# The last two blocks' down projection by two levels of seven products

## The chip, the cores and the metric

The kernel runs on one core of one Trainium2 chip. The metric is the device time of one execution in microseconds (us). TensorE (PE; PEld is its weight load), VectorE (DVE), ScalarE (ACT), GpSimd (POOL) and the queue engine SyncE (SP) each work through their own list of instructions and wait for each other by semaphores.

## The reference

The kernel computes a linear attention followed by a gated feed-forward block, all in float32:

```
kv  = einsum('bhsd,bhse->bhde', k, v)            # 8 batches, 8 heads, 576 rows, 64 wide
o   = einsum('bhsd,bhde->bhse', q, kv)
o   = o / sqrt(mean(o*o, -1) + 1e-6) * g_norm
x   = o as (4608 tokens, 512)
g   = x @ w_gate                                 # 512 x 1536
out = (g * sigmoid(g) * (x @ w_val)) @ w_out     # 1536 x 512
```

The product with `w_gate` and `w_val` is called *up* here, the one with `w_out` *down*; `h` is what lies between them.

## The kernel before, in words

The 4608 tokens are cut into nine blocks of 512. Blocks 0, 1 and 2 go alone; blocks 3 to 8 go in three pairs (`Pair`), of which 7 and 8 are the last. The attention of later blocks is worked in between, so that in the last pair nothing but up and down is left.

**Products by seven.** A 2 x 2 split of both factors needs seven products of half the size in place of eight, at the price of sums of the parts (the form of Winograd, whose parts are named S1, S3 and so on in the code). The seven are numbered 1, 5, 6, 2, 7, 4, 3. `CHAIN` says into which bank of PSUM each one accumulates: 1, 6, 7 and 4 run on one after the other in a bank of pool b, 2 has one in a, 5 and 3 share one in c. After every product the state of its bank is copied or added into SBUF, and the next product of the chain may only then overwrite it. Pool b has three banks, c two, a one, m two.

**Up of a pair** uses two levels, 49 products per column j of `h` (six columns, `NP`), for both blocks at once. The outer seven are taken in four groups (`Inner.GROUPS`: (1,5), (6,2), (7), (4,3)), and each group runs the inner seven in the order of `Inner.sequence`, with two products of the group before among its own. An inner product of a group of two is two matmuls of 128 x 128 weights against 256 columns (128 tokens of each block). VectorE adds it into SBUF, or ScalarE copies it (`Inner.multiply`, matmul at L816, copies at L830). `made1` to `made3` make the outer sums on POOL, the Silu on ScalarE (L845, L862), and `h` by two multiplications on POOL (L132 through `mul`), for the last column on VectorE. `Ffn.h_sums` then makes the sums of `h` that down needs, on POOL, for the first block of the pair. The names `add`, `sub` and `mul` stand in L130, L131 and L132, so all sums of the kernel have one of these lines.

**Weights of up** are made ready during blocks 1 and 2, written to DRAM as `w`, and read back by `Stream` (L906, SP queue) into `t` tiles, nine of 256 KB, each about as long ahead as tiles come free.

**Down** uses one level, block after block (`Down`, matmul at L661, the last product's at L1032 through `third`). Here `h` is held as weights and `w_out` (`wo`) is moved: a product is 12 matmuls of 128 x 128 against 256 columns, and the result has tokens in its rows, as `out` wants it. Three of the seven need differences of parts of `wo`, which POOL makes into `t` tiles (`turn_t`). For the last pair (`down.lone`) the order is 1, 5, 6, 2, 7, 3, 4, and for the very last block (`final`) results are added and stored in halves, so that the last piece is small. Stores are issued on SP (L1122).

**What sets the order.** The code is traced once, and a scheduler orders each engine's instructions, as a rule in the order of the code, but with those moved ahead that are ready before others. `tc.issue_after` and `in_order(engines)` tie it down; down of a pair stands in `in_order(nc.tensor.engine)`, so only TensorE's order is fixed there.

Of the kernel before, what the change touches and what calls it, by code (L numbers as in the profile page):

```python
# [18 lines left out]
def kernel(  # L19
# [620 lines left out]
    class Quad:  # L640


        def __init__(self, steps):
            self.steps = steps
            self.ps, self.room = {}, None

            self.apart = {}

# [3 lines left out]
        def multiply(self, p):  # L652
            name, first = CHAIN[p]
            if first:
                tiles = [PSUMS[name].tile([P, 2, HB], F32, name=name) for _ in range(1 + (name in self.apart))]
                self.ps[name], self.apart[name] = tiles[0], tiles[-1]
            banks = self.ps[name], self.apart[name]
            for e, i in self.order(p):
                lhsT, rhs = self.operands(p, e, i)

                self.ffn.multiplied = nc.tensor.matmul(  # L661
                    banks[e][:, e], lhsT=lhsT, rhs=rhs, start=first and i == 0 and (e == 0 or banks[0] is not banks[1]),
                    stop=i == self.steps - 1, skip_group_check=True,
                )
            getattr(self, f"after{p}", lambda: None)()
# [91 lines left out]
    class Inner:  # L757
# [94 lines left out]
        def made3(self, p, e, q):  # L852
# [7 lines left out]
            mul(engine, h[:, :, :, 0:HB], halves(c11), halves(c12))  # L860
            with tc.issue_after(self.ffn.fifth.ins):
                nc.scalar.activation(out=c21, in_=c21, func=ACT.Silu)  # L862
            mul(engine, h[:, :, :, HB:BLK], halves(c21), halves(c22))
            self.ffn.ended = self.ffn.a.h_sums(self.j, 1, engine)

# [13 lines left out]
    class Stream:  # L879
# [15 lines left out]
        def pump(self):  # L895

            while self.next and not self.held[-9]:
                n, j, c = key = self.next.pop(0)
                tile_ = t_tile(key)
                os, ps = JOINT[c]  # L900
# [6 lines left out]

        def use(self, n, j, o, p):
            c, i = self.joint[o, p]
            key = n, j, c  # L910
# [74 lines left out]
    class Down(Quad):  # L985
        def __init__(self, ffn):
# [3 lines left out]
            self.final = ffn.n == NB - 1  # L990
            self.lone = False
            self.opens = None
            self.keeps = False
            if self.final:
                self.apart["c"] = None
# [16 lines left out]
        def multiply(self, p, es=(0, 1)):  # L1012
            if p == 3 and self.lone:
                self.third(es)
                return
# [7 lines left out]
        def third(self, es):  # L1023


            if es[0] == 0:
                tiles = [m_psum.tile([P, 2, HB], F32, name="m") for _ in range(1 + self.final)]
                self.thirds = tiles[0], tiles[-1]
            for e in es:
                for i in range(self.steps):  # L1030
                    lhsT, rhs = self.operands(3, e, i)
                    self.ffn.multiplied = nc.tensor.matmul(  # L1032
                        self.thirds[e][:, e], lhsT=lhsT, rhs=rhs, start=i == 0 and (e == 0 or self.final),
                        stop=i == self.steps - 1, skip_group_check=True,
                    )
            if not self.final:
                add(nc.vector, self.o1[:, :, HD:DM], self.thirds[0], self.u2)
                self.ffn.store(self.o1, 0)
                return
            for e in es:  # L1040
                add(nc.vector, self.o1[:, e, HD:DM], self.thirds[e][:, e], self.u2[:, e])
                self.ffn.store(self.o1[:, e : e + 1, HD:DM], e, slice(HD, DM))

        def after6(self):
            super().after6()
            if self.lone:
                self.add_c(self.u2, self.u2)

        def order(self, p):
            order = [(e, i) for e in range(2) for i in range(self.steps)]  # L1050
            return order if p == 3 and self.final else sorted(order, key=lambda ei: ei[1])
# [17 lines left out]
        def rows(self):  # L1069
            o = ring()  # L1070
            self.o1, self.o2 = o[:, 0:2], o[:, 2:4]

        def after2(self):
            if self.lone:
                self.rows()
            add(nc.vector, self.o1[:, :, 0:HD], self.ps["a"], self.s)
            if self.final:
                self.ffn.store(self.o1[:, :, 0:HD], 0, slice(0, HD))
# [4 lines left out]
        def after7(self):  # L1083
            if not self.lone:
                self.rows()
            u3 = self.piece(2)
            nc.scalar.copy(out=u3, in_=self.ps["b"])
            self.add_c(self.o2[:, :, HD:DM], u3)
# [5 lines left out]
        def after3(self):  # L1094
            self.add_c(self.o1[:, :, HD:DM], self.u2)
            if not self.final:
                self.ffn.store(self.o1, 0)
                return
            for e in range(2):
                self.ffn.store(self.o1[:, e : e + 1, HD:DM], e, slice(HD, DM))  # L1100

        def add_c(self, o, u):

            if not self.final:
                add(nc.vector, o, self.ps["c"], u)
                return
            for e, c in enumerate((self.ps["c"], self.apart["c"])):
                add(nc.vector, o[:, e], c[:, e], u[:, e])

    class Ffn:  # L1110
# [9 lines left out]
        def store(self, o, t, columns=slice(None)):  # L1120
            rows = out[BLK * self.n : BLK * (self.n + 1), columns].rearrange("(t p) d -> p t d", t=T)
# [40 lines left out]
        def down(self, nxt, then={}):  # L1162
# [3 lines left out]
            down.lone = nxt is None  # L1166
            order = (1, 6, 5, 7, 2, 4, 3) if 5 in fill else (1, 5, 6, 7, 2, 4, 3)
            if down.lone:
                order = (1, 5, 6, 2, 7, 3, 4)
            for p in order:  # L1170
# [305 lines left out]
```

## Time and profile before

| | us |
|---|---|
| median of 3 runs | 1013.13 |
| lowest, highest | 1012.27, 1013.3 |
| the profiled execution, its own time | 1012.7 |
| span of its instructions | 1010.9 |
| last pair, up | 808 to 934.6 |
| last pair, down | 934.6 to 1007.6 |
| PE busy in the span | 993.7 |
| DVE, ACT, POOL busy in the span | 673.7, 232.2, 369.6 |

The span runs from the first to the last instruction; the execution's own time is 1.8 us longer. The granted clock of TensorE is 1.0 throughout. One float32 matmul leaves two records, so counts of matmul records are twice the number of matmuls in the code. A line of a group gives the line in the code, the engine, the operation, what is written and read, the shape and the count, then busy time and mean duration in ns, then the idle time just before and what ended it. A row of busy time by stretches gives the stretch, its length, and the busy time of PE, PEld, DVE, ACT and POOL, with the number of instructions in brackets, then granted clock, share of the DMA engines and GB/s.

### The profile page before, as it was taken

To read this page: it belongs to the slowest core of one execution; us is meant where nothing else is said; L and a number is where in the kernel's file an instruction comes from. 1 tells how busy PE (TensorE), PEld (TensorE's weight loads), DVE (VectorE), ACT (ScalarE), POOL (GpSimd) and SP (SyncE) were. 2 spreads that over 40 slices of the span, in tenths; PEclk is the share of its full clock that TensorE was granted. 3 is DMA by queue.
4 is the path that set the end of the run, shared out by engine and by line. 5 is a ranking of instruction groups with operands and counts; after the bars stand their busy time and mean duration, and the time that the engine had idled before them with its cause. 6 is when DMAs were issued, how large, how long until landed. Compare 5 with 4: busy or idle time off the path is not lost.

```text
span 1010.9 us, 17078 instructions
## 1 busy us (share of the span) xinstructions
PE 993.7 (98%) x6506; PEld 831.6 (82%) x6506; DVE 673.7 (67%) x1121; ACT 232.2 (23%) x367; POOL 369.6 (37%) x290
## 2 busy tenths in 40 slices
PE   5999999999999999999999999999999999999998
PEld 4544688888888888888888888888888888888887
DVE  2999797589868477656676746666668566666311
ACT  2665111221122311212211121121112121121000
POOL 0000263255544240445456004455660026546600
PEclk9999999999999999999999999999999999999999
DMA  8688653483866855767742464667221654553011
GB/s 220 198 266 260 120 93 136 97 288 97 210 136 122 214 114 158 189 179 182 170 130 42 111 164 135 182 164 191 77 42 43 146 164 144 150 145 101 1 42 42
DMA packets 254290, 143.23 MB, mean 142 GB/s; under 512 B 149504, under 2 KB 236544, under 8 KB 254208
## 3 DMA queue, kind: packets, MB, share of 16 engines
q1 hardware_dynamic: 223488, 138.20, 50.8%
q10 hardware_dynamic: 30656, 3.94, 2.5%
q8 instruction: 52, 0.85, 0.4%
q14 instruction: 30, 0.25, 0.1%
q0 software_dynamic: 64, 0.00, 0.0%
HBM read 104.99 MB, written 28.70 MB: 132 GB/s over the span
## 4 chain that ended last, share of the span: by engine, by line
PE 75%; DMA 1%; POOL 0%; SPq 0%; issue 0%; DVE 0%; POOLq 0%
PE b L816 22%; PE b L661 20%; PE c L816 11%; PE c L661 9%; PE a L816 5%; PE a L661 5%; PE m L431 1%; PE m L1032 1%; PE m L370 1%; DMA ld<-in_v_dram 1%; POOL t L131 0%; SPq L312 0%; PE b L370 0%; PE b L431 0%; PE a L431 0%
## 5 line engine op out<-in xcount | busy, mean ns | idle before, releaser
L816 PE MATMUL b<-arena,t 128*128 128x256 f32 x1008 | 244.5, 381 | 0.0
L816 PEld LDWEIGHTS b<-arena,t 128*128 128x128 f32 x1008 | 190.1, 190 | 29.6 <-DVE r L130 2.4
L130 POOL TENSOR_TENSOR r<-r 128x256 f32<-128x256 f32 (+1 forms) x90 | 94.7, 1054 | 246.1 <-DVE r L130 154.9
L130 DVE TENSOR_TENSOR r<-b,r 128x512 f32<-128x512 f32 (+1 forms) x234 | 138.9, 606 | 60.1 <-PE b L816 54.8
L130 DVE TENSOR_TENSOR r<-c,r 128x512 f32<-128x512 f32 (+1 forms) x170 | 104.5, 623 | 81.9 <-PE c L816 40.1
L132 POOL TENSOR_TENSOR arena<-r 128x1024 f32<-128x1024 f32 (+1 forms) x54 | 102.1, 1904 | 112.3 <-DVE r L130 67.9
L131 POOL TENSOR_TENSOR t<-wo 128x512 f32<-128x512 f32 x54 | 76.9, 1445 | 167.8 <-DVE wo L130 105.9
L130 DVE TENSOR_TENSOR r<-a,r 128x512 f32<-128x512 f32 x93 | 59.2, 636 | 108.3 <-PE a L661 70.7
L816 PE MATMUL c<-arena,t 128*128 128x256 f32 x504 | 122.5, 379 | 0.0
L131 DVE TENSOR_TENSOR arena<-arena 128x512 f32<-128x512 f32 (+3 forms) x96 | 104.3, 1101 | 20.0 <-PE b L661 17.7
L816 PEld LDWEIGHTS c<-arena,t 128*128 128x128 f32 x504 | 95.6, 190 | 13.5 <-issue 0.3
L661 PE MATMUL b<-wo,arena 128*128 128x256 f32 x432 | 98.1, 382 | 0.2
L661 PE MATMUL b<-t,arena 128*128 128x256 f32 x432 | 96.2, 379 | 0.0
L661 PEld LDWEIGHTS b<-wo,arena 128*128 128x128 f32 x432 | 81.2, 190 | 12.5 <-DVE arena L132 0.9
L661 PEld LDWEIGHTS b<-t,arena 128*128 128x128 f32 x432 | 82.1, 190 | 11.2
L830 ACT COPY r<-b 128x512 f32<-128x512 f32 x54 | 31.7, 586 | 189.9 <-PE b L816 189.9
L131 POOL TENSOR_TENSOR t<-arena 128x512 f32<-128x512 f32 x36 | 51.1, 1432 | 56.2 <-PE c L661 21.9
L816 PE MATMUL a<-arena,t 128*128 128x256 f32 x252 | 66.1, 379 | 0.0
L816 PEld LDWEIGHTS a<-arena,t 128*128 128x128 f32 x252 | 47.9, 190 | 6.5
L661 PE MATMUL c<-t,s 128*128 128x256 f32 x216 | 48.1, 379 | 0.0
L661 PE MATMUL a<-wo,arena 128*128 128x256 f32 x216 | 48.1, 379 | 0.0
L661 PEld LDWEIGHTS a<-wo,arena 128*128 128x128 f32 x216 | 41.0, 190 | 5.6
(115 smaller groups left out, 1242.9 us busy)
## 6 DMA issues: line engine op xcount, KB each, us to landing
t<-w SPq DMA_DIRECT2D x180, 256.0 KB, 3.1
out_dram<-r SPq DMA_DIRECT2D x17, 512.0 KB, 2.9
ld<-in_k_dram SPq DMA_DIRECT2D x26, 288.0 KB, 4.6
ld<-in_v_dram SPq DMA_DIRECT2D x26, 288.0 KB, 6.1
t<-w SPq DMA_DIRECT2D x54, 128.0 KB, 2.3
ld<-in_moe_w_gate_dram SPq DMA_DIRECT2D x12, 512.0 KB, 4.6
ld<-in_moe_w_val_dram SPq DMA_DIRECT2D x12, 512.0 KB, 4.7
ld<-in_moe_w_out_dram SPq DMA_DIRECT2D x12, 512.0 KB, 4.8
```

Of the source, the lines that this page charges most:

```text
L130: add = lambda e, o, a, b: e.tensor_tensor(out=o, in0=a, in1=b, op=OP.add)
L131: sub = lambda e, o, a, b: e.tensor_tensor(out=o, in0=a, in1=b, op=OP.subtract)
L132: mul = lambda e, o, a, b: e.tensor_tensor(out=o, in0=a, in1=b, op=OP.mult)
L370: self.positions = nc.tensor.matmul(self.kv_ps[r][u * D : (u + 1) * D, g, :], lhsT=k[:, u, c, :], rhs=v[:, u, c, :], start=(c == 0), stop= ...
L431: self.multiplied = nc.tensor.matmul(self.ps[i][u][p : p + D, t, j, :], lhsT=self.qt[rows, tile_t, head, p : p + D], rhs=kvs[b % 3][rows, ...
L661: self.ffn.multiplied = nc.tensor.matmul(banks[e][:, e], lhsT=lhsT, rhs=rhs, start=first and i == 0 and (e == 0 or banks[0] is not banks[1 ...
L816: self.ffn.multiplied = nc.tensor.matmul(ps[:, i], lhsT=stream.use(self.ffn.n, self.j, o, p), rhs=self.operand(o, p), start=first and i == ...
L830: copied = nc.scalar.copy(out=dst, in_=ps)
L1032: self.ffn.multiplied = nc.tensor.matmul(self.thirds[e][:, e], lhsT=lhsT, rhs=rhs, start=i == 0 and (e == 0 or self.final), stop=i == self ...
```

## The change

Down of the last pair is done by two levels for both blocks at once, in the manner of up: 49 products of three matmuls, with a 128 x 128 part of `wo` (or a difference of such parts) as the weights and 128 tokens of each block, 256 columns, moved. The result has the columns of `out` in its rows and tokens along them, and must be turned back.

- *During up of the last pair* VectorE makes the parts of `wo`, by `Deep.tick`, one step after every second product: 6 sums inside `wo` (512 elements in each of 128 partitions), 12 differences for the outer products 1, 2, 6, 3 into `ld` tiles (384 elements), and for the outer products 5, 7, 4 three sets each, of three differences (512, 128 and 256 elements) in one buffer, written to DRAM as `leaf` on SP (448 KB a set).
- *The sums of `h`* are made for both blocks on POOL as columns come out (`Deep.made`), and the inner ones of two columns at a time on VectorE (`turn`). The second half of the last column is put off into down (`second`).
- *Down* (`Deep.down`) writes out by hand the order of products `m(group, inner)`, of the sums for the inner level (`sum_x`, 768 elements each) and the outer level (`outer`, 768 each), and of the results. The groups are (1,2), (6,5), (7), (4,3). It stands in `in_order` for TensorE and VectorE both.
- *Leaf weights* are read back through `Stream`, 192 KB a product, after the pair's own.
- *Turning back.* Two of the four quarters of the result are turned by VectorE in blocks of 32 x 32 and placed by 16 DMAs each of 128 B pieces (`send`), one quarter on ACT's queue and one on SP's. The other two are turned by 16 TensorE transposes in four steps (`turn_back`), copied by ScalarE (the last one by both) and stored.
- *Gone:* `apart`, `final`, `lone`, `third` and `add_c`, which served the old last pair alone.

The diff, cut to its core:

```diff
+            if self.ffn.deep:
+                self.ffn.deep.made(self.j, engine, c21, halves(c21), halves(c22), h)
+                return
...
+    class Last(Inner):
+        GROUPS = ((1, 2), (6, 5), (7,), (4, 3))
...
+            for c in cs:
+                for i, o in enumerate(self.outers):
+                    self.ffn.multiplied = nc.tensor.matmul(
+                        ps[:, i], lhsT=self.deep.weight(o, p, c), rhs=self.deep.operand(o, p, c),
+                        start=first and c == 0 and i == 0, stop=c == 2, skip_group_check=True,
+                    )
...
+            if p in self.ADDED:
+                add(nc.vector, dst, ps, dst)
+            elif self.g == 3:
+                add(nc.vector, dst, ps, self.shared[2][:, :, :, e, q])
+            elif self.g == 0:
+                nc.scalar.copy(out=dst, in_=ps)
+            else:
+                add(nc.vector, dst[:, 0], ps[:, 0], self.onto[:, :, e, q])
+                if n > 1:
+                    nc.scalar.copy(out=dst[:, 1], in_=ps[:, 1])
...
+            for i, o in enumerate(self.LEAVES):
...
+                        lambda b=b, rows=rows, raw=raw: sub(nc.vector, raw, b[:, rows], self.quadrant(6)[:, rows]),
+                        lambda: sub(nc.vector, temp[:, 4], temp[:, 0], temp[:, 1]),
+                        lambda: sub(
+                            nc.vector, temp[:, 5:7], temp[:, 2:4], temp[:, 1:2].to_broadcast([P, 2, P])
+                        ),
+                        lambda i=i, c=c: nc.sync.dma_start(out=self.dram[:, i, c], in_=temp[:, 0:7]),
...
+        def tick(self):
+            self.count += 1
+            if self.later and self.count % 2 == 0:
+                self.later.pop(0)()
+
+        def made(self, j, engine, c21, g, v, h):
+            def second():
+                mul(engine, h[:, :, :, HB:BLK], g, v)
+                a11, a21, a22 = h[:, :, 0, 0:HB], h[:, :, 0, HB:BLK], h[:, :, 1, HB:BLK]
+                add(engine, a21, a21, a22)
+                sub(engine, a21, a21, a11)
...
+            if j == NP - 1:
+                self.second = second
+                return
+            second()
+            if j % 2:
+                self.later[0:0] = self.turn(j // 2, (0, 1))
...
+        def down(self):
...
+            run(self.turn(2, (0,)))
+            m(0, 1, (0, 1))
+            m(0, 2, (0, 1))
+            m(0, 1, (2,))
+            self.sum_x(0, 1, 2)
+            m(0, 2, (2,))
+            m(0, 6)
+            self.sum_x(1, 1, 2)
+            m(0, 5)
+            self.sum_x(2, 1, 2)
+            m(0, 7)
+            self.second()
+            run(self.turn(2, (1,)))
+            self.outer(5, ((0, 0),))
+            m(0, 3)
+            self.outer(5, ((0, 1),))
+            m(1, 1)
...
+            m(2, 5)
+            add(nc.vector, c11, p1, c11)
+            nc.vector.transpose(out=room[:, 0], in_=c11)
+            self.send(room[:, 0], 0, 0, nc.scalar)
+            self.outer(3)
+            m(2, 2)
+            m(2, 7)
...
+            add(nc.vector, v, u2, c22)
+            self.sum_x(0, 4, 3)
+            m(2, 3)
+            m(3, 1)
+            self.sum_x(1, 4, 3)
+            m(2, 4)
+            m(3, 6)
+            self.sum_x(2, 4, 3)
+            m(3, 5)
+            add(nc.vector, c22, u3, c22)
+            nc.vector.transpose(out=room[:, 1], in_=c22)
+            self.send(room[:, 1], 1, 1, nc.sync)
+            m(3, 2)
+            m(3, 7)
...
+            self.turn_back(0, 0)
+            m(3, 3)
+            self.turn_back(1, 1)
+            m(3, 4)
+            self.turn_back(1, 0)
+            self.turn_back(0, 1, True)
...
+        if pair.deep:
+            stream.leaves(pair.deep)
+            pair.up(fill)
+            with in_order(nc.tensor.engine, nc.vector.engine):
+                pair.deep.down()
+            continue
```

## The prediction

> **What bounds the kernel now.** I read the page first, then busy time by stretches for the two stages that the change rewrites, then the chain of waits, then the groups and the timeline for the prices.
>
> ```profile
> PE 993.7 (98%) x6506; PEld 831.6 (82%) x6506; DVE 673.7 (67%) x1121; ACT 232.2 (23%) x367; POOL 369.6 (37%) x290
> ```
>
> TensorE is busy for all but 17 us of the span. The busy time by stretches puts the last pair's up stage in the first row and its down stage in the second:
>
> ```profile
> 808.00:934.60 126.60, 126.60 (x586) 110.91 (x586) 84.66 (x144) 25.71 (x35) 65.54 (x53) 1.00 0.47 141
> 934.60:1007.60 73.00, 72.94 (x338) 63.86 (x337) 16.46 (x21) 5.75 (x9) 16.54 (x13) 1.00 0.07 26
> ```
>
> The columns after the length are PE, PEld, DVE, ACT, POOL. PE never idles in either. In up, VectorE already works 84.7 of 126.6 us and POOL 65.5; in down both have nearly nothing to do. The chain of waits ends so:
>
> ```profile
> 999.77 5.18 PE b L661 x24
> 1004.95 2.60 PE m L1032 x12
> 1007.55 0.02 issue
> 1007.58 0.42 DVE r L130
> ```
>
> One down product is 12 matmuls (24 records) in 5.18 us, **0.432 us per matmul** of 256 columns. Fourteen products are 168 matmuls, 72.6 us of the 72.9 us between 934.64 and 1007.55. Every matmul taken out is therefore worth 0.432 us, provided that VectorE, which gets the new sums, keeps up.
>
> **The prices of VectorE and POOL.** Groups of the up stage, shapes apart:
>
> ```profile
> L130 DVE TENSOR_TENSOR r<-b,r 128x512 f32<-128x512 f32 x53 | 36.6, 691 | 15.2 <-PE b L816 13.9 <-PE a L816 0.5
> L130 DVE TENSOR_TENSOR r<-b,r 128x256 f32<-128x256 f32 x24 | 10.0, 416 | 0.6
> L132 POOL TENSOR_TENSOR arena<-r 128x1024 f32<-128x1024 f32 x10 | 23.4, 2363 | 19.0 <-DVE r L130 19.0
> ```
>
> [...] One behind the other, starts in this trace lie closer: 0.33 us for 256 elements, 0.60 for 512, 1.14 for 1024; so 0.87 for 768[...].
>
> [...] in the up stage of block 1:
>
> ```profile
> 221.88 0.29 DVE L130 TENSOR_TENSOR t<-t 128x128 f32<-128x128 f32 x1
> 222.21 1.70 DVE L131 TENSOR_TENSOR r<-t 128x256 f32<-128x256 f32 x2
> 222.21 1.54 POOL L132 TENSOR_TENSOR arena<-r 128x512 f32<-128x512 f32 x1 [2.18 <-DVE t L130]
> 223.72 1.31 POOL L131 TENSOR_TENSOR t<-wo 128x512 f32<-128x512 f32 x1
> 223.83 1.35 DVE L131 TENSOR_TENSOR t<-t 128x128 f32<-128x128 f32 x1
> ```
>
> The same 128-element subtract takes 0.29 us free and 1.35 us behind POOL's 1.31. Adds that read PSUM and one SBUF tile stay at 0.69 whatever POOL does. [...]
>
> **Down, part by part.** *Removed:* 168 matmuls. *Added:* 49 products of 3 matmuls, 147 x 0.432 = 63.5 us, and 16 TensorE transposes; those of block 0 (L494) start every 0.11 us, so 1.7 us. Bare sum 65.2, **7.7 us less** than 72.9. Against it stand VectorE's own sums. They are 33 of 768 elements (21 in sum_x, 12 in outer: 28.7 us), evacuations of about 12 us, two transposes (L386's 1024-element one: 1.23), seven sums or products of 1024 elements or pairs of 512: some 54 us, against 16.5 before. Both engines' order is fixed here, so a late sum stops TensorE. Walking the written order with these prices, three places don't fit:
> - After product (0,7) VectorE does its evacuation, the postponed second half of h (1024, 512, 512), two turns of 512 and the first outer sum: 0.2+0.6+1.2+4x0.69+0.96 = 5.7 us. TensorE has only product (0,3), 2.6 us, before (1,1) needs that sum: **3.1 us** idle.
> - From product (2,5) to the evacuation of (3,1) VectorE has 0.33+1.14+1.23+4x0.87+2x0.33+1.14+2x0.87+0.33+0.69 = 10.7 us, and 0.2 to start; TensorE has (2,2), (2,7), (2,3), (2,4) at 1.3 and (3,1) at 2.6, 7.8 us, before (3,6) may overwrite that bank: **3.1 us**.
> - The last turn back waits for the last add: 0.9 us less one 0.44 us turn: **0.5 us**; then a copy of 0.42 as before.
>
> The start of down is covered: h of the last column is there 0.2+0.69+1.2 = 2.1 us after up's last product, and eight matmuls that need only the columns j = 0 to 3, 3.5 us, stand before it; without that cover it would be 2.1 us. What VectorE did in down before (two subtracts of 1536 per block, the old results' adds: 16.5 us) goes, and was hidden: 0.
>
> Down is 65.2+6.7 = 71.9 us, so **-1.0**. Both ends: -4 if half of the idle time is covered, +3 if dependent sums cost more.
>
> *Moved past queues:* the two sends are 16 DMAs each of 256 pieces of 128 B. The nearest row is a q load of 32 to 48 KB on SP:
>
> ```profile
> L333 SPq DMA_DIRECT2D ld<-in_q_dram x240: 311/451/2144, 100.6 to 703.2; - x120
> ```
>
> At 0.45 us, one send holds its queue for 7.2 us. ACT's send lies where ACT has no copy due. SP's starts about 10 us before the end, with seven row stores behind it (0.38 each): just in time, so 0, with 0 to +3 as bounds (L522's larger ones took 0.6 to 1.1). The 21 leaf loads, 192 KB each, use nine tiles ahead of at least 1.3 us of work each: hidden; uncovered it would be their 2.8 us to landing, once. POOL's subtracts for down (turn_t) go: they were hidden, 0.
>
> **Up.** Its 294 matmuls stay. VectorE gets 49 SBUF-only instructions: 6 of 512, 12 of 384, nine times 512+128+256, and four of 1024: about 24 us, which fits into 42 us of idle time by the average. But steps are popped every second product until two thirds of the stage are over; those 85 us have some 28 us free. [...] Per column j, 21.2 us, POOL has three instructions of 2.36, four of 0.73, and two sums that grow from 0.73 to 1.27 as they take both blocks. A random arrival waits (3x2.36²+4x0.73²+2x1.27²)/(2x21.2) = 0.52 us. Some ten instructions can go before POOL's first work of the stage; the other 39 wait 20 us in all. 24+20 exceeds 28: the queue fills, and evacuations stand behind it. Product 6 may follow 1 over two others, 1.73 us; less 0.2 and the evacuation's 0.69, **0.84 us** is the slack. An instruction that meets a 2.36 us one waits 1.2 on average and works 0.6, thus overruns by 0.9. Long ones fill a third of the time: 13 hits, of which I take half as standing before an evacuation that is due, 6 us. The turns of 1024, in two pairs, take 2.3 us and meet POOL's product on top: 1.5 to 4 each, 4 us together (one pair may fall into a slack place). I take **+9**; the ends are +3 (sums happen to fall between POOL's work) and +17.
>
> A further wait: the nine leaf sets share one buffer, and a 448 KB write of it (3 to 4.5 us by the rows for 384 and 512 KB) must end before the next set. In this stage the order isn't fixed, and instructions are moved forward when ready: POOL's L131 t<-wo, written last in the stage, runs at 926 before L130 adds written earlier. So I take the wait at 0, in the ends 0 to 1 us per set.
>
> **Sum.** 1012.7 (profiled execution, span 1010.9) - 1.0 + 9 = 1020.7; the runs' median is 0.4 above that execution: **1021 us**.
>
> **Rivals.** 0.2% of the time, 2 us, is about what a measurement can tell from no change.
> - *Likeliest, 0.77, slower:* [...] 1015.5 to 1031. Within it, 0.12 for the extreme: sums run in their written order, and the write of the leaf buffer holds VectorE: 8 waits of 2 to 3 us more, 1031 and above.
> - *Covered, 0.12, no change:* up grows by 1 to 3 us only: 1011 to 1015.
> - *Not slower, 0.11:* up hides all 49. The place is the slack of 0.84 us: 18 of them (2 x 512 per chunk, then 384s) are ready from the start, when POOL is idle for 11 us and ScalarE takes most evacuations; the rest falls between POOL's long products. Then -1.0 counts, and with half of down's idle time covered, -4: 1009. It decides once up grows by less than about 1 us and down keeps under 69 us. For it: 42 us free on the average. [...]
> - *It doesn't do what it says:* rows leave late behind SP's send; +3 on any of these.
>
> The range, 1012 to 1031, takes in down's and up's ends and leaves out some 0.2.
>
> **What would show it.** Right: the chain's L816 part has gaps on PE after VectorE in up, [...] up of 130 to 144 us; in down two PE gaps near 3 us before (1,1) and (3,6), matmul records from 336 to about 310. Wrong: up still 127 us; or gaps behind DMA leaf; or down longer than 75 us.

## The result, and the profile after

The kernel after takes **1036.42 us** (median of 4 runs, 1034.76 to 1037.63) against 1012.7 for the kernel before on the same chip: a ratio of 1.0234, 95% interval 1.0214 to 1.0254. It is slower, as predicted, but by 23.7 us and not by 8, and it lies above the predicted range. The profiled execution took 1037.63 us; its span is 1035.5.

In the kernel after the lines have moved: the up matmul is L813 (L816 before), the old down matmul L658, the new one L889, the transposes that turn back L1065, the copies after them L1068, L1069 and L1071, the sends L1056, the row stores L1076. The sums stay at L130 to L132.

The busy times on the page, to be set beside the first line that the prediction shows:

```profile
PE 995.5 (96%) x6480; PEld 829.4 (80%) x6480; DVE 738.9 (71%) x1222; ACT 233.4 (23%) x371; POOL 357.9 (35%) x275
```

TensorE has 26 records fewer and yet more busy time, and idles 40 us in place of 17. Busy time by stretches for the two stages (columns as before: length, then PE, PEld, DVE, ACT, POOL, granted clock, share of DMA, GB/s):

```profile
810.00:955.90 145.90, 135.08 (x590) 114.84 (x590) 111.74 (x193) 25.68 (x35) 70.33 (x50) 0.95 0.52 160
955.90:1028.30 72.40, 66.40 (x311) 57.11 (x309) 54.41 (x71) 6.65 (x12) 0.00 (x0) 1.00 0.24 56
```

Up has TensorE idle for 10.8 us, and busy for 8.5 us longer at a granted clock of 0.95, for the same matmuls. VectorE went from 84.7 to 111.7 us there. Down has 311 records for 338 and TensorE idle for 6.0 us, where it had none. The chain of waits ends so; its last steps run through a transpose and two copies:

```profile
1024.18 2.61 PE b L889 x12
...
1026.81 0.70 DVE r L130
...
1027.65 0.65 PE m L1065 x4
...
1028.32 0.43 DVE r L1068
...
1028.78 0.37 ACT r L1069
```

The last of these ends at 1029.15, and the span goes on to 1035.5. I call that stretch, from the last busy engine to the span's end, the tail. Taking up from its first matmul to down's first, and down to TensorE's last work:

| us | before | after | change |
|---|---|---|---|
| up starts at | 807.6 | 810.0 | +2.4 |
| up | 127.3 | 145.9 | +18.6 |
| down | 72.7 | 72.4 | -0.3 |
| last copies | 0.5 | 0.9 | +0.4 |
| tail | 2.9 | 6.35 | +3.45 |
| span | 1010.9 | 1035.5 | +24.6 |

The start of up lies between 805.6 and 810.0 us in all kernels of this study. VectorE's first sums inside `wo` stand before it (from 805.91 us), but TensorE waits for none of them, and two kernels below with the same up start at 807.3 and 807.5; so I count that row as scatter. The **up stage holds three quarters of the loss, the tail most of the rest**.

**The up stage.** The timeline around its longest gap (start, length, engine, line, operation, tiles; in brackets the idle time before, and what ended it):

```profile
860.94 2.80 POOL L132 TENSOR_TENSOR arena<-r 128x1024 f32<-128x1024 f32 x1
...
863.82 1.26 POOL L130 TENSOR_TENSOR arena<-arena 128x512 f32<-128x512 f32 x1
865.16 1.26 POOL L131 TENSOR_TENSOR arena<-arena 128x512 f32<-128x512 f32 x1
866.46 1.23 DVE L130 TENSOR_TENSOR arena<-arena 128x1024 f32<-128x1024 f32 x1 [4.92 <-POOL arena L131]
867.60 0.68 DVE L130 TENSOR_TENSOR r<-c,r 128x512 f32<-128x512 f32 x1
...
868.34 1.22 PE L813 MATMUL c<-arena,t 128*128 128x256 f32 x2 [4.45 <-DVE r L130]
```

The instruction at 866.46 is the first half of `turn`. It needs the sums of h that POOL finishes at 866.42, and VectorE stands before it for 4.92 us. Behind it stands an evacuation of bank c, and TensorE waits 4.45 us for that bank. This is a wait for data at the head of an engine's list. The second turn does the same at 918.35 (VectorE 4.14 us, TensorE 2.87). And then the clock falls:

```profile
864.90:868.30 3.40, 0.00 (x0) 0.00 (x0) 1.84 (x3) 0.00 (x0) 1.44 (x2) 0.99 0.06 21
868.30:875.00 6.70, 6.16 (x14) 4.46 (x15) 4.62 (x8) 0.00 (x0) 1.45 (x2) 0.50 0.07 20
875.00:880.00 5.00, 5.00 (x25) 4.42 (x24) 4.76 (x10) 1.06 (x1) 1.45 (x2) 1.00 0.27 62
919.40:926.20 6.80, 5.97 (x14) 4.61 (x15) 5.50 (x10) 0.00 (x0) 1.95 (x3) 0.50 0.02 5
```

From 868.2 to 875.0 us TensorE is granted half its clock, and 14 records take 6.16 us where 25 take 5.0 right after. The same follows the second turn, from 919.4 to 926.2. The half clock lasts 6.8 us each time. The gap before it was 4.45 us the first time and 2.87 us the second; which gaps the clock followed is worked out below, with the row stores.

The waits for POOL that the prediction reckoned with are there too. Groups of the up stage, shapes apart:

```profile
L131 DVE TENSOR_TENSOR ld<-wo 128x384 f32<-128x384 f32 x12 | 8.0, 692 | 0.0
L131 DVE TENSOR_TENSOR s<-wo 128x512 f32<-128x512 f32 x9 | 7.3, 815 | 5.8 <-DMA leaf<-s 5.8
...
L131 DVE TENSOR_TENSOR s<-s 128x256 f32<-128x256 f32 x9 | 5.3, 583 | 0.0
...
L131 DVE TENSOR_TENSOR s<-s 128x128 f32<-128x128 f32 x9 | 4.5, 500 | 0.0
```

Where no POOL instruction runs beside them, these four take about 0.55, 0.69, 0.42 and 0.28 us in this trace; the longest that meets one takes 2.19, 1.22, 0.96 and 1.25. The means are 0.14, 0.12, 0.17 and 0.22 us over the free times; times the counts, about 6 us in all. Where such a sum stands before an evacuation, TensorE idles too, as here behind a sum of 128 elements that took 1.25 us:

```profile
840.14 1.25 DVE L131 TENSOR_TENSOR s<-s 128x128 f32<-128x128 f32 x1
...
842.04 1.13 PE L813 MATMUL b<-arena,t 128*128 128x256 f32 x4 [1.03 <-DVE r L130]
```

So the trace divides the 18.6 us of up. The gaps behind the turns (4.45, 0.51 and 2.87 us) are 7.8. The clock is about 6.1, half of the 12.1 us that TensorE is busy in the two slow stretches. The gaps behind the small sums (1.03, 0.79 and 1.17) are 3.0. The remaining 1.7 us are too short to be named one by one.

**Down** has the two gaps of the prediction, before products (1,1) and (3,6):

```profile
974.80 0.70 PE L889 MATMUL b<-arena,t 128*128 128x256 f32 x2 [2.73 <-DVE arena L130]
...
1010.09 0.70 PE L889 MATMUL b<-arena,t 128*128 128x256 f32 x2 [2.24 <-DVE r L130]
```

The 0.96 us for a sum of 768 elements in the walk to the first of them was my estimate; the 33 sums of this size took 0.95 us each here.

**The tail** is the SP queue (SPq, ACTq: a queue's own issues; the length covers all of its count):

```profile
1018.71 7.75 SPq L1056 DMA_DIRECT2D out_dram<-r  x16
...
1026.55 6.37 SPq L1076 DMA_DIRECT2D out_dram<-r  x7
```

The second send holds the queue until 1026.46, and the seven row stores behind it leave until 1032.92, 3.8 us after the last copy.

### The profile page after: what moved, and what is told of

The parts are those of the page before. It is cut to its first block, busy times and chain, and to the rows that moved or that the text cites. A ratio compares the mean times of both kernels' runs of the same rounds, so it can differ in the third digit from the quotient of the medians.

```text
span 1035.5 us, 17216 instructions
## 1 busy us (share of the span) xinstructions
PE 995.5 (96%) x6480; PEld 829.4 (80%) x6480; DVE 738.9 (71%) x1222; ACT 233.4 (23%) x371; POOL 357.9 (35%) x275
## 4 chain that ended last, share of the span: by engine, by line
PE 66%; DVE 3%; DMA 3%; POOL 1%; issue 1%; SPq 1%; ACT 0%; DVEq 0%; POOLq 0%
PE b L813 18%; PE b L658 15%; PE c L813 9%; PE c L658 8%; PE a L813 4%; PE a L658 4%; PE b L889 3%; DMA leaf<-s 1%; PE c L889 1%; DVE r L130 1%; DMA t<-w 1%; PE m L431 1%; SPq L312 1%; PE m L370 1%; PE a L889 1%
## 5 line engine op out<-in xcount | busy, mean ns | idle before, releaser
L813 PE MATMUL b<-arena,t 128*128 128x256 f32 x1008 | 247.9, 385 | 3.1 <-DVE r L130 3.0
L813 PEld LDWEIGHTS b<-arena,t 128*128 128x128 f32 x1008 | 192.0, 192 | 35.1 <-DVE r L130 7.1
L130 DVE TENSOR_TENSOR r<-b,r 128x512 f32<-128x512 f32 (+1 forms) x247 | 145.5, 602 | 67.2 <-PE b L813 50.8
L130 POOL TENSOR_TENSOR r<-r 128x256 f32<-128x256 f32 (+1 forms) x90 | 96.0, 1068 | 259.0 <-DMA t<-w 151.4
L130 DVE TENSOR_TENSOR r<-c,r 128x512 f32<-128x512 f32 (+1 forms) x171 | 105.4, 625 | 53.1 <-PE c L813 32.7
L132 POOL TENSOR_TENSOR arena<-r 128x1024 f32<-128x1024 f32 (+1 forms) x54 | 103.5, 1930 | 113.4 <-DVE r L130 67.0
L813 PE MATMUL c<-arena,t 128*128 128x256 f32 x504 | 126.1, 387 | 8.6 <-DVE r L130 7.8
L131 DVE TENSOR_TENSOR arena<-arena 128x512 f32<-128x512 f32 (+5 forms) x119 | 121.4, 1041 | 9.2 <-PE b L658 6.9
L130 DVE TENSOR_TENSOR r<-a,r 128x512 f32<-128x512 f32 x95 | 60.2, 634 | 91.6 <-PE a L658 65.9
L131 POOL TENSOR_TENSOR t<-wo 128x512 f32<-128x512 f32 x45 | 64.1, 1446 | 165.1 <-DVE wo L130 106.7
L813 PEld LDWEIGHTS c<-arena,t 128*128 128x128 f32 x504 | 97.0, 194 | 24.0 <-DVE r L130 10.3
L658 PE MATMUL b<-wo,arena 128*128 128x256 f32 x336 | 76.8, 383 | 0.2
L658 PE MATMUL b<-t,arena 128*128 128x256 f32 x336 | 74.8, 379 | 0.0
L658 PEld LDWEIGHTS b<-wo,arena 128*128 128x128 f32 x336 | 63.0, 190 | 9.9 <-DVE arena L132 0.8
L658 PEld LDWEIGHTS b<-t,arena 128*128 128x128 f32 x336 | 64.0, 190 | 8.6
L131 POOL TENSOR_TENSOR t<-arena 128x512 f32<-128x512 f32 x36 | 51.1, 1433 | 56.7 <-PE c L658 22.4
L813 PE MATMUL a<-arena,t 128*128 128x256 f32 x252 | 66.7, 381 | 0.0
L813 PEld LDWEIGHTS a<-arena,t 128*128 128x128 f32 x252 | 48.3, 192 | 6.5
L130 DVE TENSOR_TENSOR arena<-arena 128x512 f32<-128x512 f32 (+4 forms) x46 | 39.9, 884 | 9.5 <-POOL arena L131 9.1
L658 PE MATMUL b<-arena 128*128 128x256 f32 x192 | 45.5, 380 | 0.0
L658 PE MATMUL b<-arena,t 128*128 128x256 f32 x192 | 45.4, 379 | 0.0
```

What stands on the lines that cost most here:

```text
L130: add = lambda e, o, a, b: e.tensor_tensor(out=o, in0=a, in1=b, op=OP.add)
L131: sub = lambda e, o, a, b: e.tensor_tensor(out=o, in0=a, in1=b, op=OP.subtract)
L132: mul = lambda e, o, a, b: e.tensor_tensor(out=o, in0=a, in1=b, op=OP.mult)
L658: self.ffn.multiplied = nc.tensor.matmul(ps[:, e], lhsT=lhsT, rhs=rhs, start=first and i == 0 and e == 0, stop=i == self.steps - 1, skip_g ...
L813: self.ffn.multiplied = nc.tensor.matmul(ps[:, i], lhsT=stream.use(self.ffn.n, self.j, o, p), rhs=self.operand(o, p), start=first and i == ...
```

## The experiments

Each is the kernel after with one edit, if nothing else is said. Up, down and tail are read as in the table.

**The turns are held back by a column.** They are issued behind a later evacuation, so that POOL is done with what they need.

```diff
-            if j % 2:
-                self.later[0:0] = self.turn(j // 2, (0, 1))
+            if j in (2, 4):
+                def held(step):
+                    with tc.issue_after(self.pair.added.ins):
+                        step()
+                self.later[0:0] = [lambda step=step: held(step) for step in self.turn(j // 2 - 1, (0, 1))]
```

> Only the two turns of h in up (two VectorE instructions of 1024 elements each) are moved: each pair stands one column later in VectorE's order, so that POOL's sums, for which they wait, are long done. Theory A (VectorE's order puts the turns ahead of evacuations while POOL is not done, and TensorE's clock falls to half after the gap): the gaps of 4.4 and 2.9 us at 868 and 920 go, and with them the two stretches of 6.8 us at half clock; up falls from 145.7 to about 131 us, the time from 1036.4 to 1022. Theory B[...]: the turns meet POOL's products elsewhere, up falls by 4 us at most, 1032 or more. Theory C (the leaf buffer's DMA): no more than 6 us, since its waits stay.

Measured: 1027.12 us, ratio 1.0153 (1.0136 to 1.0171). Up 136.9 (145.9 in the kernel after), no half clock in it, tail 6.6. So holding the turns back wins **9 us** and frees the clock, and 9.6 us of loss remain; the 131 us of theory A were not reached. For now the turns meet POOL's product instead, as the timeline shows:

```profile
877.61 5.65 POOL L132 TENSOR_TENSOR arena<-r 128x1024 f32<-128x1024 f32 x2 [4.65 <-DVE r L130]
...
877.98 3.07 DVE L130 TENSOR_TENSOR arena<-arena 128x1024 f32<-128x1024 f32 x1
...
882.30 1.99 PE L813 MATMUL b<-arena,t 128*128 128x256 f32 x8 [2.29 <-DVE r L130]
```

The turn takes 3.07 us in place of 1.23, and the gap on TensorE is 2.29 us. With three shorter ones (0.50, 1.31 and 0.80) the gaps behind the held turns are 4.9 us. The 14 us behind the turns in the kernel after, less these 4.9, are the 9 us won.

**The leaf sums left out, the leaf transfers kept.**

```diff
-                        lambda b=b, rows=rows, raw=raw: sub(nc.vector, raw, b[:, rows], self.quadrant(6)[:, rows]),
...
+                        lambda: None, lambda: None, lambda: None,
+                        lambda i=i, c=c, plain=plain: nc.sync.dma_start(out=self.dram[:, i, c], in_=plain[:, 0:7]),
```

> Leaves out the 27 differences for the outer products 5, 7 and 4 (the leaf DMAs write plain rows of w_out in their place, same bytes and places). VectorE loses 27 of its 49 added instructions in up and all waits for the leaf buffer; the turns stay. Theory A: the two turns' gaps and the half clock stay, so only the gaps at 842, 891 and 895, 3 us together, go: 1032 to 1034. Theory B and C: most of the 19 us that up grew by goes: 1020 to 1025.

Measured: 1028.72 us, ratio 1.0168 (1.0151 to 1.0185). Up is 139.1 with VectorE at only 99.1 us busy, and TensorE's two gaps of 2.87 us stand behind the turns, at a stage clock of 0.96. A VectorE with 12.7 us less to do still loses 11.8 us of up against before, and the only gaps left are behind the turns (2.87, 2.87 and 0.60 us, with 10.2 us at half clock). The time lies between the two forecasts; nearly all that remains is the four turn instructions.

**Row stores on ACT's queue**, all but one.

```diff
-                queue = nc.scalar if final and o else nc.sync
+                queue = nc.sync if final and not o else nc.scalar
```

> Only the row stores of turn_back change queue: all but one of the last step's go out on ACT, so that none stands behind the 16 DMAs that the second send issues on SP from 1018.7 to 1026.5. Theory A as said of the tail (SP is late by some 4 us at the end): the time from VectorE's last copy to the end falls from 6.8 to about 3 us, 1036.4 to 1032.5. If the late end is the slow transfer of 128 B pieces and not the issue, nothing changes.

Measured: 1034.96 us, ratio 1.0228 (1.0213 to 1.0244), which alone can't be told from the kernel after. In the trace the tail is 3.2 us, against 6.35, 6.6, 5.4 and 5.4 in the kernels with the stores on SP (this change, and those with the turns held, the leaf sums left out, and the sums on POOL). So the queue is worth 2 to 3.5 us. Down was longer in this run, 75.8 us for 72.4, which hid most of it in the time, and the reason is the clock. Down has the same two gaps as in the kernel after (2.74 and 2.24 us), but here each is followed by 3.4 us at half clock, about 1.7 us lost. The first two rows are this run's, around its first gap; the third is the kernel after, where the clock stayed:

```profile
969.51:972.92 3.41, 0.84 (x4) 0.77 (x5) 3.34 (x6) 0.00 (x0) 0.00 (x0) 1.00 0.00 0
972.92:976.33 3.41, 3.41 (x10) 2.70 (x9) 0.94 (x3) 0.00 (x0) 0.00 (x0) 0.50 0.00 0
...
970.60:974.01 3.41, 1.47 (x7) 0.95 (x5) 3.27 (x6) 0.00 (x0) 0.00 (x0) 1.00 0.00 0
```

Here it went with where a gap lies. In the trace of the kernel after, the stretches at half clock start at 868.20, 919.40 and 1032.04 us: 51.20 and 112.64 us apart, 15 and 33 times 3.413. Cut into windows of 3.413 us that start at these times, that trace has, from 60 us on, three windows at full clock in which TensorE idles for 2.04 us or more (from 915.99 us for 2.04, from 864.79 and 1028.63 for the whole 3.41), and each is followed by half the clock. In the 277 others at full clock it idles for 1.95 us or less, and none is. In the rows above it idles for 2.57 and for 1.94 us. The same gap (2.74 us here, 2.73 in the kernel after) can thus cost the clock or not. Six of the runs with this down (this one, the turns held, the leaf sums left out, the sums on POOL, and the two variants of the held turns below) have half clock in it and take 74.1 to 75.8 us; the kernel after, with 72.4, was spared.

**One long VectorE instruction in the kernel before**, of 4096 and of 6144 elements, in the middle of the last up.

```diff
+                if i == 9 and self.n + 2 == NB:
+                    flat = wo.rearrange("p f d -> p (f d)")[:, 0:4096]
+                    with tc.issue_after(self.added.ins):
+                        nc.vector.tensor_tensor(out=flat, in0=flat, in1=flat, op=OP.max)
```

> The kernel before with one VectorE instruction of 4096 elements (about 4.4 us, it keeps w_out as it is) behind an evacuation in the third column of the last up. It measures what one late VectorE instruction costs there. TensorE should idle some 3.5 to 4 us. If the clock falls to half after it, as at 868 and 920 in the changed kernel, 3.4 us more are lost in 6.8 us: 1012.7 to about 1020. If the clock is not a part of it: 1016.5.

> As e4_long, with 6144 elements, 6.6 us in place of 4.4. The gap of TensorE should grow by the difference, from 1.6 to 3.7 us. If such a gap lets the clock fall to half, as at 868 and 920 in the changed kernel, a stretch of 3.4 or 6.8 us at half clock follows and the kernel before becomes slower by 5.4 to 7.1 us, about 1018; without it by 3.7 us, 1015.7.

Measured, the short one: 1014.44 us, ratio 1.0025 (1.0015 to 1.0036); the long one: 1019.84, ratio 1.0069 (1.0049 to 1.0088). The two timelines, the short one first:

```profile
860.98 4.42 DVE L1246 TENSOR_TENSOR wo<-wo 128x4096 f32<-128x4096 f32 x1
...
865.78 0.70 PE L816 MATMUL b<-arena,t 128*128 128x256 f32 x2 [1.56 <-DVE r L130]
```

```profile
861.98 6.55 DVE L1246 TENSOR_TENSOR wo<-wo 128x6144 f32<-128x6144 f32 x1
...
868.92 0.70 PE L816 MATMUL b<-arena,t 128*128 128x256 f32 x2 [3.70 <-DVE r L130]
```

The gap of 1.56 us (3.5 to 4 were expected) leaves the clock at 1.0, and up grows by 1.9. After 3.70 us the clock is at half for 3.4 us, and up grows by 6.3 (127.3 to 133.6): 2.1 us more of instruction cost 4.4 us more of stage. In this place TensorE rides over some 2.8 us of a VectorE that is away (4.42 less 1.56, 6.55 less 3.70); beyond that each us counts once as a gap, and a gap long enough also in the clock.

**The leaf sums and the turns on POOL** (`nc.gpsimd` in place of `nc.vector` in both).

> The 27 differences for the leaf weights and the four turns in up are made by POOL and no longer by VectorE; all else as in the changed kernel. VectorE's instructions with two SBUF inputs in up are then only the 18 at its start, before POOL has work[...], and no turn stands in its way. Theory A (what up lost is VectorE held by POOL: half of it by waiting for POOL's sums at the turns with the clock's fall after it[...]): up falls from 145.8 to 128 to 130 us, no stretch at half clock in it, the time to about 1019. Rival D (POOL, then busy for some 105 of 127 us, delivers the outer sums late and TensorE waits for it): up stays over 135 us, with gaps that end by VectorE adds which waited for POOL.

Measured: 1033.98 us, ratio 1.0199 (1.0174 to 1.0224); up 143.6. Now VectorE waits for POOL. From the waits of the up stage (us in total, times, longest):

```profile
POOL s L131 <- DMA leaf<-s: 15.6, 7, 4.5
...
DVE r L130 <- POOL r L130: 12.6, 5, 6.4
```

This is rival D: POOL is late with the outer sums; one such wait of 6.4 us makes a gap of 5.6 us on TensorE, and the clock falls for 6.8. The work moved to POOL takes the wait with it: POOL is now busy for 100.6 us of the stage, in place of 70.3.

**The turns held, and no wait for the leaf buffer.** The transfers read `wo` in place of the buffer, which VectorE may then overwrite at once.

```diff
-                        lambda i=i, c=c: nc.sync.dma_start(out=self.dram[:, i, c], in_=temp[:, 0:7]),
+                        lambda i=i, c=c, plain=plain: nc.sync.dma_start(out=self.dram[:, i, c], in_=plain[:, 0:7]),
```

> As e1_turn_late, but the leaf DMAs send plain rows of w_out and not the buffer of the differences, which are still made (the leaf weights are left out of the result so). The buffer's reuse then waits for no DMA. If these waits (7.4 us of VectorE in e1) hold TensorE, up falls from 136.9 to about 131 us. [...] within 2 us of 136.9, since the gaps at 838, 861, 882 and 927 follow instructions that stood behind POOL and not behind a DMA.

Measured: 1033.96 us, ratio 1.0205 (1.0183 to 1.0226); up 140.7, 3.8 us **longer** than with the turns held alone, where VectorE waited 7.4 us for the leaf transfers. Without that wait the sums come earlier and fall on POOL's products:

```profile
833.91 4.70 POOL L132 TENSOR_TENSOR arena<-r 128x1024 f32<-128x1024 f32 x2 [5.49 <-DVE r L130]
...
834.28 2.13 DVE L131 TENSOR_TENSOR s<-s 128x128 f32<-128x128 f32 x1
...
836.94 1.96 DVE L131 TENSOR_TENSOR s<-s 128x256 f32<-128x256 f32 x1
...
839.55 2.93 PE L813 MATMUL b<-arena,t 128*128 128x256 f32 x6 [4.06 <-DVE r L130]
```

A sum of 128 elements takes 2.13 us where it takes 0.28 free. Two of them within one product pair of POOL cost a gap of 4.06 us, and half a clock for 3.4 us behind it. Both forecasts, 131 us and within 2 us of 136.9, missed: taking the wait for the transfer away does not shorten up, it moves the sums to worse places.

**The turns held, and the leaf sums made by instructions with one SBUF input** (transposes of the same sizes).

```diff
-                        lambda: sub(nc.vector, temp[:, 4], temp[:, 0], temp[:, 1]),
+                        lambda: nc.vector.transpose(out=temp[:, 4], in_=temp[:, 0]),
```

> As e1_turn_late, but each of the 27 leaf differences is replaced by a VectorE transpose of 32 x 32 blocks of the same number of elements, one SBUF input in place of two (the leaf weights are left out of the result so). Length and order on VectorE, and the waits for the DMA, stay[...]. [...] these instructions keep 0.3, 0.4 and 0.7 us, the gaps at 838 and 861 (1.0 and 1.4 us) go, up falls by 2.5 to 4 us to about 133.5, and what is left are the gaps at the turns. If the number and length of VectorE's instructions are the cause: up stays at 136 to 137.

Measured: 1025.4 us, ratio 1.0126 (1.0108 to 1.0144), up 137.0. All 27 transposes keep their time (0.69 to 0.71, 0.29 to 0.30 and 0.39 to 0.44 us for the three sizes), two of them here inside POOL's products, while the turns, with two inputs, do not:

```profile
831.68 4.68 POOL L132 TENSOR_TENSOR arena<-r 128x1024 f32<-128x1024 f32 x2 [4.75 <-DVE r L130]
...
833.80 0.71 DVE L957 STREAM_TRANSPOSE s<-wo 128x512 f32<-128x512 f32 x1 [0.47 <-DMA leaf<-s]
...
835.61 0.29 DVE L958 STREAM_TRANSPOSE s<-s 128x128 f32<-128x128 f32 x1
...
876.61 5.64 POOL L132 TENSOR_TENSOR arena<-r 128x1024 f32<-128x1024 f32 x2 [6.26 <-DVE r L130]
...
876.99 3.06 DVE L130 TENSOR_TENSOR arena<-arena 128x1024 f32<-128x1024 f32 x1
...
881.30 2.68 PE L813 MATMUL b<-arena,t 128*128 128x256 f32 x8 [3.88 <-DVE r L130]
```

So inside POOL's products the instructions with one SBUF input kept their time (0.71 us for 512 elements and 0.29 for 128), and the one with two took 3.06 us where it takes 1.23 free. The gaps of 1.04 and 1.37 us that stood behind the small sums with the turns held are gone but for 0.27, as the first forecast had it. But up is no shorter, since one turn on POOL's product now makes a gap of 3.88 us in place of 2.29, and the clock falls for 3.4: what was won at the sums was lost again at a turn.

**Down in another order, and the stores on ACT's queue.** The sums of products 5 and 3 go by single quarters between evacuations, those of 7 in two halves; (0,7) and (0,3) stand behind the last product of h, and the first send comes later.

```diff
-            m(0, 7)
             self.second()
             run(self.turn(2, (1,)))
             self.outer(5, ((0, 0),))
-            m(0, 3)
+            m(0, 7)
             self.outer(5, ((0, 1),))
+            m(0, 3)
+            self.outer(5, ((1, 0),))
             m(1, 1)
+            self.outer(5, ((1, 1),))
...
+            self.outer(3, ((0, 0),))
             m(1, 4)
+            self.outer(3, ((0, 1),))
             m(2, 6)
+            self.outer(3, ((1, 0),))
             m(2, 5)
-            add(nc.vector, c11, p1, c11)
-            nc.vector.transpose(out=room[:, 0], in_=c11)
-            self.send(room[:, 0], 0, 0, nc.scalar)
-            self.outer(3)
+            self.outer(3, ((1, 1),))
```

> The change with its down written in another order (the VectorE sums for product 5 and 7 split into single quarters and set between evacuations, product (0,7) and (0,3) moved past the last product of h, product 3's quarters begun one product pair earlier, the first row block sent three products later), and with all but one of the last row stores on ACT's queue; the up is that of the change. Theory: the two gaps of 2.7 and 2.2 us in the down are VectorE standing before its sums, so the down falls from 72.4 to about 66 us, the end after the last engine work from 6.35 to about 3.2 us as with the stores alone, and the time from 1036.4 to about 1027 us (ratio to before 1.014 to 1.017). Rival, products wait on VectorE's total work in the down and not on its order: gaps move to other products, down stays at 71 to 74 us and the time is 1033 us (ratio 1.020).

Measured: 1025.82 us, ratio 1.0134 (1.0119 to 1.0149). Up is unchanged, 145.7; the tail 4.05 (3.2 was expected; three stores now stand behind ACT's last copy). Down is 66.1, and up to 1017.7 us its row is:

```profile
953.10:1017.70 64.60, 64.60 (x305) 56.69 (x304) 53.87 (x70) 6.07 (x11) 0.00 (x0) 1.00 0.26 61
```

TensorE does not idle in these 64.6 us, with the same work on VectorE (53.9 us, 54.4 before the reorder); the last turn back adds 1.5. Against the 72.7 us of the old down, the second level is worth 6.6 us once VectorE's order lets it be.

**VectorE's order in up written by hand**, on top of the last kernel: the 45 differences at chosen products, and the turns at products 109, 139, 150 and 165 of 168.

```diff
+        SLOTTED = [0, 0, 0, 0, 0, 0, 0, 4, 8, 9, 10, 12, 18, 22, 24, 25, 27, 28, 28, 28, 29, 38, 40, 43, 52, 56, 57, 66, 71, 76, 83, 84, 85, 95, 102, 104, 111, 113, 113, 122, 127, 130, 139, 140, 141]
+        TURNS = [109, 139, 150, 165]
...
-            pair.up(fill)
+            with in_order(nc.vector.engine):
+                pair.up(fill)
```

> The down and the stores as in the run sent beside it; in addition VectorE's instructions of the last up keep the order in which they are written, each of the 45 weight-difference instructions stands at a slot of its own among the 168 products (thinner where GpSimd works its products and sums), and the two turns of h stand at slots 109 and 139 (first two channel blocks) and 150 and 165 (next two), behind GpSimd's work that they need. Theory that the up's loss is VectorE standing on GpSimd[...] and the clock that falls with the gap: most of the 18 us goes, the up takes 128 to 133 us with no gap over 2 us and no half clock in it, and the time is 1007 to 1013 us (ratio 0.995 to 1.001). Rival, VectorE's added busy time of itself fills the up: the up stays at 136 us or more, as with the held turns, and the time is 1016 us or more (ratio 1.004 and over).

Measured: **1009.59 us**, ratio 0.9978 (0.9967 to 0.9988), 2.4 us or 0.2% faster than the kernel before. Up, and down to 1000.0 us (all of down is 66.9), by stretches:

```profile
807.30:934.50 127.20, 126.69 (x585) 110.54 (x584) 114.39 (x192) 25.69 (x35) 70.76 (x50) 1.00 0.60 183
934.50:1000.00 65.50, 65.50 (x309) 57.59 (x309) 55.10 (x73) 6.06 (x11) 1.65 (x1) 1.00 0.26 61
```

Up takes what it took before the change, with VectorE **busier** than in the kernel after (114.4 for 111.7 us). The longest gap in it is 0.37 us.

**The same, with the differences at every second product again** (slots 1, 3, 5 and so on to 105).

> The run e10_order with one thing put back: the 45 weight-difference instructions stand at every second product again (from slot 1 to slot 105, as in the change), not at chosen slots; VectorE's written order, the turns' slots, the down and the stores are as in e10_order. Theory that two separate causes cost the up, the turns (about 9 us with the clock) and the even spread beside GpSimd's products and leaf transfers (about 9 us): only the turns are cured, the up takes about 135 to 137 us as with held turns and the time is 1016 to 1019 us (ratio to before 1.004 to 1.007). Rival, the written order of VectorE and the turns' slots alone cure it and the slots of the differences are indifferent: up 127 to 129 us and the time 1009 to 1011 us (ratio 0.997 to 0.999).

Measured: 1018.52 us, ratio 1.0065 (1.005 to 1.0081). Up, and one of the places:

```profile
806.00:944.00 138.00, 131.00 (x586) 108.78 (x586) 116.51 (x192) 25.69 (x35) 71.27 (x50) 1.00 0.55 169
```

```profile
883.50 4.86 POOL L132 TENSOR_TENSOR arena<-r 128x1024 f32<-128x1024 f32 x2 [4.35 <-DVE r L130]
...
883.87 2.27 DVE L131 TENSOR_TENSOR s<-s 128x256 f32<-128x256 f32 x1
...
886.79 2.43 PE L813 MATMUL b<-arena,t 128*128 128x256 f32 x10 [1.66 <-DVE r L130]
```

Eleven gaps of 0.1 to 1.7 us, clock at 1.0, up 10.7 us longer than with the chosen slots (8.9 us between the medians). So an **even spread is a cause of its own, and here about as large as what holding the turns back won**. It is no measure of its share in the kernel after, where VectorE's order in up was another and the gaps behind small sums were 3.0 us. It can't be told from this pair how much of it is waiting beside POOL's products and how much the leaf transfers, for which VectorE waits 8.9 us here and in no wait of 0.4 us or more with the chosen slots.

**Two row stores on SP**, those of quarter (1,0), in the kernel with the chosen slots.

```diff
-                queue = nc.sync if final and not o else nc.scalar
+                queue = nc.sync if (final and not o) or (e, q) == (1, 0) else nc.scalar
```

> The run e10_order with the two row stores of quarter (1,0) on SP's queue in place of ACT's. Theory that the end hangs on the row stores that ACT issues behind its last copy (three from 1002.04 us, 1.99 us of issue): two of them leave on SP from about 1001.1 us, ACT's last leaves at about 1002.4 us, and the span's end after the last engine work goes from 4.35 to about 3.2 us, the time to about 1008.5 us (ratio to before 0.996 to 0.998). Rival, the last transfer's own latency sets the end and not the issue before it: no change, 1009.6 us (ratio 0.998).

Measured: 1007.5 us, ratio 0.9956 (0.9944 to 0.9969). ACT's last store now leaves behind its copy, but the tail only goes from 4.35 to 3.9 us, and it is 4.05 and 4.0 in the two other kernels with the stores as in the one it is compared with. The intervals of the two ratios touch. So a gain from this edit is not shown, and the 2 us between the medians are not explained.

## Why the prediction was wrong, step by step

- **Down, -1.0: right.** -0.3 measured, with both places of idle time where the walk of the order put them (2.73 and 2.24 us for 3.1 each) and 0.44 for the last turn back's 0.5. The kernel after was lucky in one thing, which the sum did not hold: its gaps left the clock at 1.0, while in six other runs the same gaps cost 1.7 to 3.4 us of it. The idle time was VectorE's order and no limit of it: the reorder gave 6.3 us (72.4 to 66.1).
- **Up, +9: the step that failed**, +18.6 measured. The turns and the clock behind them are 14 us, where the sum had 4.
  - *The turns, 4 us together, priced as meetings with POOL's products.* In the kernel after they never met one: they stood at the head of VectorE's list until POOL's two sums of h were done. The gaps behind them are 7.8 us, and with the clock 14; holding them back won 9 of these (145.9 to 136.9). The text took "instructions are moved forward when ready" for the whole stage. But that is settled when the program is made: in the trace the evacuation at 867.60 us stayed behind the turn that had waited 4.92 us. The right question for the turns was what each needs and when POOL ends it.
  - *The clock: missing.* Both gaps were followed by 6.8 us at half clock, some 3 us lost each. A gap was priced at its own length.
  - *The waits for POOL and the full queue, 6 us.* In the kernel after, 4.7 us of the 18.6 are left for it, 3.0 of them gaps behind small sums: the size was near, but not by its working, an estimate that let each sum wait for the rest of the POOL instruction it met: 20 us of waits, where about 6 are measured. (The two lines that it calls the same 128-element subtract are an add, L130, and a subtract, L131.) What decides is not the sum of these waits. By the same reckoning (durations over their free ones, the turns included) the kernel with chosen slots has about 10 us of such waits and no loss in up, that with even slots about 13 and loses 10.7. The reading that fits is that an overrun costs while an evacuation is due, and is free in a slack place; no run varies that alone.
- **Leaf buffer, 0: not a cause by itself.** The waits are there (5.8 us in the kernel after), but removing them, with the turns held, made up longer by 3.8 us. As part of the even spread it stays open.
- **SP's send, 0 with a bound of +3: at the bound.** +3.45 in the tail; with the stores on ACT 3.2 us of 6.35 are left. The walk had the send end "just in time", at the last copy. It ended 2.7 us before that copy's end, but the seven stores behind it took 0.91 us of issue each on average where 0.38 was reckoned, 6.4 us in all, and the data of the first four had been copied while it was still issuing.
- **The rivals.** "Covered" and "not slower" fell as written. The latter's outcome, an up that hides all the added work, is what the chosen slots then reached, though with about 10 us of waits at POOL still in it: it was possible, and it didn't come of itself. The extreme of the likeliest case reached the right time by luck, since its cause, 16 to 24 us of waits for the leaf buffer, was 5.8.
- **What would show it**: gaps on PE behind VectorE in up, both gaps in down and 311 records came as said. Up, at 145.9, lies above the 130 to 144 named there.

## What to carry to other kernels

Where an engine keeps its written order, as VectorE did here, ask of each added instruction what it waits for and what stands behind it: 9.1 us of waiting at the head of VectorE's list cost 14 us of the stage, and 30 us of added work cost nothing once each piece had a place chosen for it. A gap on TensorE is to be priced with the clock that may follow it: gaps of 2.24 us and more were followed here by 3.4 or 6.8 us at half clock in some places. And before a transfer is put last on a queue, count the issues that already stand there.

## What was not expected of the hardware

- The length of a gap alone did not decide on TensorE's clock. After down's gaps of 2.73 and 2.24 us it stayed at 1.0 in the kernel after; after the same gaps (2.74 and 2.24) it was at 0.5 for 3.4 us each with the row stores on ACT's queue. In the trace of the kernel after, half the clock came after each window of 3.413 us with 2.04 us or more of idle time, and after none with 1.95 or less. Two gaps of 2.87 us in one run (the leaf sums left out) cost 6.8 and 3.4 us of half clock.
- A VectorE instruction with two SBUF inputs that met one of POOL's products of 2.36 us took up to most of its length on top: 128 elements in 2.13 us for 0.28, 256 in 2.27 for 0.42, 1024 in 3.07 for 1.23, some 1.85 us each. Transposes of 128 and 512 elements took 0.29 and 0.71 inside such products, as in the rest of that run.
